# Registers one expert at a time, turns in banks of their own, and one schedule as written

## The chip, the cores and the metric

The kernel runs on one core of a Trainium2 chip. The metric is the device time of one execution in microseconds.

## What is computed

Attention in chunks of 64 tokens, then a layer with 8 experts of which each token takes one, then a layer with 4 experts that all tokens pass, weighted. All in float32:

```python
attn = softmax(q_c @ k_c.T / sqrt(64)); out = attn @ v_c   # 2 x 8 heads x 9 chunks of 64
x = out as (1152, 512)
expert_idx = argmax(x @ w_gate)                            # 8 experts, capacity 288 each
disp[e, place] = x[i]                                      # i in order, dropped when full
y = relu(disp @ w1) @ w2                                   # 512 -> 1024 -> 512, per expert
out[i] = gate_w[i] * y[expert_idx[i], pos[i]]              # kept tokens
h = relu(x @ w1[e]); out += p[:, e] * (h @ w2[e])          # second layer, 4 experts, all tokens
```

## The kernel before

**Numbers.** Every float32 product is made of three products of a high part and a low part (`hl`, `xt`, `ht`: [0] high, [1] low). ACT makes the high part by a cast, DVE the low one by a subtraction (for weights `part_hi`, L115, and `part_lo`, L119).

**Attention** (L125 to L449). Tokens go in 9 tiles of 128; the loop over `j` (L323) works on stages of four tiles at once: scores of tile j, weights and values of j−1, the transposed x and logits of j−2, the rank of j−3. `fetch` (L151) brings a tile's keys, queries and values from `kqv_d`: tile 0 in three transfers, each later tile in one of 768 KB. All tiles' fetches go out in order from SP's queue. `put_k` scales the keys into `kb`; ACT does so for one half of tile 2. At its end the routing (L390 to L447) works out, on DVE, how many tokens each expert keeps and where they start (`ovi`: the number kept, then for 8 places in turn the form, then the 8 offsets), the indices for the gathers (`gidx`), and `over`. `form` tells how many row blocks an expert needs. After it `warm` matmuls (L138) keep TensorE busy.

**Registers** (L548). `numbers` loads some words of a tile into registers of the engines. L551 and L552 load all of `ovi` once, `kept` and the 8 forms on every engine, the 8 offsets on ACT and DVE. Since the expert part has no order of its own at the border, its loads stand among the last operations of the routing on DVE.

**Experts** (L520 to L735). `expert(k)` calls itself for k+1 inside a condition on `form_r[k+1]` (L728, "more"). One expert has up to three row blocks, in the order w=1 (128 rows, if form > 2, L677), w=2 (64 rows, if form is 2 or 3, L682 and L683) and w=0 (128 rows, always). A `block` (L560) is: `first(0)` into bank `pg0[w]`, `first(1)` into `pg1` with `turn(0)` in its midst, `second(0)` into `y` with `turn(1)` in its midst, `second(1)`, and at the end four transposes `ty`. A turn transposes `hs`, the array's result that ACT copied out; ACT then writes the high part `ht` (L596) and DVE the low part (L597). The turns and `ty` take the two banks of tag "tp" in turn; `y` has two banks. `xprep` transposes the gathered tokens (`xr`) of the next expert between the products of block w=0, in banks `pg0[1]`, `pg0[2]` and `pg1`. `late(k)` (L639) puts four `part_lo` of this expert's last weights on DVE before the first block, and fetches the next weights into the raw tiles that they free.

With these inputs the experts at places k=0 to 5 run. Their blocks are: k=0 w=1 and 0; k=1 all three; k=2 w=0 alone; k=3 and k=4 w=2 and 0; k=5 w=0 alone.

**Second layer** (L735 to L877): 240 us to the end of the span, in which TensorE works without pause.

The order within attention is written out for all engines, and within the experts for PE, ACT, DVE and SP, each in a manual schedule of its own; at the border the two meet in an order that a scheduler chooses.

Of the kernel before, what the change touches and what calls it, by code (L numbers as in the profile page):

```python
# [9 lines left out]
F32 = mybir.dt.float32  # L10
# [8 lines left out]
ENG = mybir.EngineType  # L19

P = 128
NTOK = 1152
# [4 lines left out]
DM = H * D  # L27
KD = DM // P
# [43 lines left out]
def kernel(ctx: ExitStack, tc: tile.TileContext, kqv_d, wg, w_all, dp, cst, out, cap):  # L72
# [4 lines left out]
    assert cap <= XW  # L77

    dpool = ctx.enter_context(tc.tile_pool(name="dpool", bufs=1, space=DRAM))
    x_d = dpool.tile([NTOK, DM], F32, name="x_d")  # L80
# [44 lines left out]
    with ExitStack() as ast:  # L125
        ap_ = ast.enter_context(tc.tile_pool(name="attn", bufs=2))
        ps = ast.enter_context(tc.tile_pool(name="aps", bufs=1, space=PSUM))
        ast.enter_context(tc.manual_schedule())

# [20 lines left out]
        def fetch(i):  # L150
            if i < NT:  # L151
                kqv[i] = ap_.tile([P, 3, DM], F32, tag="kqv", bufs=KQV, name="kqv")
                if i == 0:
                    for t in range(3):
                        nc.sync.dma_start(out=kqv[i][:, t], in_=kqv_d[:, i, t])
                else:
                    nc.sync.dma_start(out=kqv[i], in_=kqv_d[:, i])
# [361 lines left out]

    with ExitStack() as est, tc.manual_schedule(engines={ENG.PE, ENG.Activation, ENG.DVE, ENG.SP}):  # L520
        hp_ = est.enter_context(tc.tile_pool(name="mh", bufs=2))
        xtp = est.enter_context(tc.tile_pool(name="mx", bufs=1))
        ps = est.enter_context(tc.tile_pool(name="mps", bufs=1, space=PSUM))

        ys2 = [ps.tile([P, DM], F32, name=f"y{j}") for j in range(2)]


        pg0 = [ps.tile([P, FH], F32, name=f"pg0{j}") for j in range(3)]
        pg1 = ps.tile([P, FH], F32, name="pg1")
        xts = [xt0, xtp.tile([P, 2 * KD * XW], F32R, name="xt1")]  # L530
        xbig = [x[:, 0:4 * KD * P].rearrange("p (a k n) -> p a k n", a=2, k=KD) for x in xts]
# [18 lines left out]

        kept, *form_r = numbers(ovi[0:1, 0:1 + NE], max_val=NTOK)  # L551
        o_r = numbers(ovi[0:1, 1 + NE:1 + 2 * NE], engines=(ENG.Activation, ENG.DVE), max_val=NTOK)  # L552
        regs = []
# [6 lines left out]
        def block(k, w, also=()):  # L560
# [4 lines left out]
            both = n < P  # L565
            y = ys2[w % 2]
            hs, ht = {}, {}
# [23 lines left out]
            def turn(h):  # L591
                tp = ps.tile([P, NF, n], F32, tag="tp", bufs=2, name="tp")
                for j in range(NF):
# [30 lines left out]
            yr = hp_.tile([P, DM], F32, tag="ys", bufs=1, name="yr")  # L624
            ty = ps.tile([P, KD, n], F32, tag="tp", bufs=2, name="tp")
            for j in range(2):
# [24 lines left out]
        def expert(k):  # L651
# [3 lines left out]
            if k == 0:  # L655
# [6 lines left out]
                for kd in range(KD):  # L662
                    xprep(0, kd, ps.tile([P, 512], F32, tag="tp", bufs=2, name="tp") if kd < 2 else (pg0[0], pg1)[kd - 2])
                for h in range(2):
# [9 lines left out]
            elif k + 2 < NE:  # L674
                gather(k + 2)
            late(k)
            with tc.If(form_r[k] > 2):  # L677
                block(k, 1)
# [20 lines left out]
            def nxt(i, kd):  # L699
                if k + 1 < NE:  # L700
                    t = pg1 if len(turns) == KD else pg0[1 + len(turns) % 2]
                    turns.append(t)
# [20 lines left out]
            block(k, 0, also)  # L723
            if k == 0:
                scatter(meta_d, [(posi[:, i:i + 1], meta[:, i]) for i in range(NT)], [])
                nc.gpsimd.dma_start(out=mcol, in_=meta_d.rearrange("(i p) c -> p i c", p=P))
# [7 lines left out]

    with ExitStack() as est, tc.manual_schedule(engines={ENG.PE, ENG.Activation, ENG.DVE, ENG.SP}):  # L735
        accp = est.enter_context(tc.tile_pool(name="accp", bufs=1))
# [132 lines left out]
        def pick_last(ws):  # L869
            if len(ws) == 1:  # L870
                return dense(ws[0])
            with tc.If(kept <= LAST + ws[0]) as few:  # L872
                dense(ws[0])
# [48 lines left out]
```

## Time and profile before

| | us |
|---|---|
| median of 3 runs | 619.68 |
| lowest and highest | 617.58, 619.73 |
| the profiled execution's own time | 620.28 |
| its span, first to last instruction | 618.1 |
| PE busy | 579.5 (94%) |
| DVE busy | 296.1 (48%) |
| ACT busy | 200.9 (32%) |
| mean granted TensorE clock | 0.975 |

The span lies 2.2 us inside the profiled execution's time. Busy shares are means over the attention (to about 60 us), the experts (to 240 us) and the second layer. A wait is put down to what came last: an engine's name with a q (DVEq, PEq) stands for its sequencer, which takes branches and sets semaphores, apart from the arithmetic. The granted clock is a share of full speed: 1.00 is 2.4 GHz, 0.50 is 1.2 GHz.

### The profile page before, as it was taken

What the parts mean: (1) busy time and instruction counts of PE and PEld (TensorE: products, weight loads), DVE (VectorE), ACT (ScalarE), POOL (GpSimd) and SP (SyncE); (2) the same over time, 40 slices, a digit from 0 to 9 for tenths busy, and PEclk for the clock granted to TensorE, in tenths of its full rate; (3) what the DMA queues carried; (4) which work ended last, traced back from release to release, by engine and by line L of the source; (5) the groups of instructions that cost most, each with busy time, mean ns of one, the idle gap of its engine ahead of it and who ended that gap; (6) DMA issues with size and microseconds to landing.
All of it is one profiled execution on the core that took longest, in us unless ns stands there. A gap on an engine that the chain in (4) does not pass through costs nothing.

```text
span 618.1 us, 8796 instructions
## 1 busy us (share of the span) xinstructions
PE 579.5 (94%) x3376; PEld 503.6 (81%) x3376; DVE 296.1 (48%) x576; ACT 200.9 (32%) x394; POOL 71.5 (12%) x63
## 2 busy tenths in 40 slices
PE   6998699998797988999999999999999999999995
PEld 3785577776676767989989989989989989989984
DVE  4897828147445376242462452452452452454221
ACT  4785237267454476111211211211211211211110
POOL 3311813202202050000000000000000000000032
PEclk8997799999898999999999999999999999999998
DMA  8782286428727176400120120120220000000022
GB/s 326 258 286 75 60 315 202 114 73 296 262 69 249 46 233 200 186 1 1 68 69 1 68 69 1 69 68 1 69 68 1 2 1 1 1 0 1 1 83 76
DMA packets 17322, 61.36 MB, mean 99 GB/s; under 512 B 2720, under 2 KB 2864, under 8 KB 16624
## 3 DMA queue, kind: packets, MB, share of 16 engines
q1 hardware_dynamic: 14544, 52.95, 25.1%
q0 software_dynamic: 2720, 7.66, 4.1%
q8 instruction: 33, 0.54, 0.4%
q14 instruction: 25, 0.20, 0.1%
HBM read 55.86 MB, written 4.75 MB: 98 GB/s over the span
## 4 chain that ended last, share of the span: by engine, by line
PE 59%; issue 1%; POOL 1%; DVE 0%; POOLq 0%
PE pg L768 30%; PE po L797 20%; PE po L816 8%; POOL out L500 1%; PE po L831 0%; DVE xr L804 0%; POOLq L872 0%; POOLq L500 0%
## 5 line engine op out<-in xcount | busy, mean ns | idle before, releaser
L768 PE MATMUL pg<-x,hl 128*128 128x384 f32 (+1 forms) x1152 | 187.5, 322 | 1.6 <-DVEq L728 1.6
L768 PEld LDWEIGHTS pg<-x,hl 128*128 128x128 f32 x1152 | 184.5, 188 | 3.1 <-issue 1.8
L797 PE MATMUL po<-hl,h 128*128 128x512 f32 (+1 forms) x588 | 137.4, 392 | 0.0
L797 PEld LDWEIGHTS po<-hl,h 128*128 128x128 f32 x588 | 108.6, 188 | 24.6
L119 DVE TENSOR_TENSOR hl<-raw,hl 128x1024 fp32r<-128x1024 f32 x80 | 95.3, 1219 | 24.0 <-ACT hl L115 20.2
L778 ACT ACTIVATE h<-pg 128x384 fp32r<-128x384 f32 x64 | 31.5, 492 | 186.1 <-PE pg L768 185.8
L115 ACT CAST hl<-raw 128x1024 fp32r<-128x1024 f32 x80 | 82.2, 1056 | 0.9 <-DVEq L728 0.9
L779 DVE SCALAR_TENSOR_TENSOR h<-pg,h 128x384 fp32r<-128x384 f32 x64 | 35.6, 557 | 94.2 <-ACT h L778 94.2
L574 PE MATMUL pg<-hl,xt 128*128 128x512 f32 x240 | 65.4, 421 | 3.2 <-PEq L682 1.6
L574 PE MATMUL y<-hl,ht 128*128 128x512 f32 x240 | 65.0, 412 | 1.6 <-DVE ht L597 1.6
L804 DVE SCALAR_TENSOR_TENSOR xr<-po,mcol,xr 128x512 f32<-128x512 f32 (+1 forms) x43 | 31.7, 737 | 59.7 <-PE po L797 59.0
L574 PEld LDWEIGHTS pg<-hl,xt 128*128 128x128 f32 x240 | 45.9, 200 | 14.6 <-issue 5.3
L574 PEld LDWEIGHTS y<-hl,ht 128*128 128x128 f32 x240 | 43.7, 192 | 13.4 <-DVE ht L597 4.4
L816 PE MATMUL po<-h,hl 128*128 128x288 f32 x384 | 51.9, 295 | 0.0
L816 PEld LDWEIGHTS po<-h,hl 128*128 128x128 f32 x384 | 51.3, 189 | 0.0
L775 ACT CAST h<-pg 128x288 fp32r<-128x288 f32 x32 | 12.8, 400 | 97.9 <-DVE pg L773 97.9
L400 POOL DMA_INDIRECT xr<-x_d,gidx x24 | 28.2, 1174 | 127.8 <-PE pg L540 95.4
L825 POOL MEMSET raw<- 128x512 f32 x1 | 0.5, 527 | 268.4 <-DVE hl L119 268.4
L597 DVE SCALAR_TENSOR_TENSOR ht<-tp,ht 128x512 fp32r<-128x512 f32 (+1 forms) x22 | 13.6, 616 | 28.5 <-ACT ht L596 28.4
L822 DVE TENSOR_TENSOR rest<-po,rest 128x288 f32<-128x288 f32 x28 | 12.8, 458 | 26.6 <-PE po L816 26.6
L773 DVE SCALAR_TENSOR_TENSOR pg<-pg,xt 128x288 f32<-128x288 f32 x32 | 22.1, 690 | 1.6 <-PE pg L768 1.6
L776 DVE TENSOR_TENSOR h<-pg,h 128x288 fp32r<-128x288 f32 x32 | 14.7, 459 | 15.4 <-ACT h L775 15.4
(158 smaller groups left out, 393.6 us busy)
## 6 DMA issues: line engine op xcount, KB each, us to landing
raw<-in_w_all SPq DMA_DIRECT2D x72, 512.0 KB, 4.1
kqv<-in_kqv SPq DMA_DIRECT2D x8, 768.0 KB, 8.1
raw<-in_w_all SPq DMA_DIRECT2D x4, 1024.0 KB, 5.7
x_d<-x SPq DMA_DIRECT2D x9, 256.0 KB, 3.1
xt<-meta_d SPq DMA_DIRECT2D x1, 1056.0 KB, 8.5
kqv<-in_kqv SPq DMA_DIRECT2D x3, 256.0 KB
xr<-x_d,gidx POOLq DMA_INDIRECT x24
cc<-in_cst SPq DMA_DIRECT2D x1, 373.5 KB
```

Source lines behind the costliest of these rows:

```text
L115: nc.scalar.copy(hls[j][:, 0, a:b], raws[j][:, a:b])
L119: nc.vector.tensor_tensor(out=hls[j][:, 1, a:b], in0=raws[j][:, a:b], in1=hls[j][:, 0, a:b].bitcast(F32), op=ALU.subtract)
L400: nc.gpsimd.indirect_dma_start(out=xrs[k % 2][0:n, w, :], out_offset=None, in_=x_d[:, :], in_offset=bass.IndirectOffsetOnAxis(ap=ix, axis=0))
L574: nc.tensor.matmul(o, t(a), wt(b), start=start and i == 0, stop=stop and i == len(pairs) - 1)
L768: nc.tensor.matmul(pg[:, 0:n], w1(u % 2, a, kd)[:, ff * P:ff * P + P], x2[:, b, kd, g * GW:g * GW + n], start=c == 0, stop=c == 3 * KD - 1)
L773: nc.vector.scalar_tensor_tensor(out=hs, in0=hs, scalar=0.0, in1=domain(u // NH), op0=ALU.max, op1=ALU.mult)
L776: nc.vector.tensor_tensor(out=h[:, ff, 1, 0:n], in0=hs, in1=h[:, ff, 0, 0:n].bitcast(F32), op=ALU.subtract)
L778: nc.scalar.activation(out=h[:, ff, 0], in_=pg[:, 0:GW], func=ACTF.Relu)
L779: nc.vector.scalar_tensor_tensor(out=h[:, ff, 1], in0=pg[:, 0:GW], scalar=0.0, in1=h[:, ff, 0].bitcast(F32), op0=ALU.max, op1=ALU.subtract)
L797: nc.tensor.matmul(po, h[:, ff, a, tt * P:tt * P + P], w2(u % 2, b, ff)[:, cols], start=c == 0, stop=c == 3 * NF - 1)
L804: nc.vector.scalar_tensor_tensor(out=acc[t][:, cols], in0=po, scalar=pe, in1=acc[t][:, cols], op0=ALU.mult, op1=ALU.add)
L816: nc.tensor.matmul(po[:, 0:W], w2(u % 2, b, ff)[:, d * P:d * P + P], h[:, ff, a, 0:W], start=c == 0, stop=c == 3 * NF - 1)
```

## The change

Line numbers of the kernel after are higher by 1 (L119 is L120) to 11.

1. One manual schedule over the whole kernel, so the border between attention and experts runs as written. POOL's manual schedule ends with the attention, as before.
2. Tile 1's keys, queries and values are fetched in three transfers of 256 KB, as tile 0's.
3. At first only `form_r[0]` is loaded, and the first offset is the number 0. `count(k + 1)`, after `late(k)`, loads one form on every engine and one offset on ACT and DVE. `kept` is loaded at the end of expert 0.
4. Three banks `tps` instead of the two rotating ones, and one `y` instead of two. The first turn and `ty` of a block take `tps[w]`, the second turn takes `pg0[w]`; `xprep` of the next expert takes `pg0[1]`, `pg0[2]`, `tps[1]`, `tps[2]`, `pg1`.

```diff
+    ctx.enter_context(tc.manual_schedule(engines={ENG.PE, ENG.Activation, ENG.DVE, ENG.SP}))
     dpool = ctx.enter_context(tc.tile_pool(name="dpool", bufs=1, space=DRAM))
...
-        ast.enter_context(tc.manual_schedule())
+        ast.enter_context(tc.manual_schedule(engines={ENG.Pool}))
...
-                if i == 0:
+                if i < 2:
                     for t in range(3):
                         nc.sync.dma_start(out=kqv[i][:, t], in_=kqv_d[:, i, t])
...
-    with ExitStack() as est, tc.manual_schedule(engines={ENG.PE, ENG.Activation, ENG.DVE, ENG.SP}):
+    with ExitStack() as est:
...
-        ys2 = [ps.tile([P, DM], F32, name=f"y{j}") for j in range(2)]
         pg0 = [ps.tile([P, FH], F32, name=f"pg0{j}") for j in range(3)]
+        tps = [ps.tile([P, 512], F32, name=f"tp{j}") for j in range(3)]
         pg1 = ps.tile([P, FH], F32, name="pg1")
+        y = ps.tile([P, DM], F32, name="y")
...
-        kept, *form_r = numbers(ovi[0:1, 0:1 + NE], max_val=NTOK)
-        o_r = numbers(ovi[0:1, 1 + NE:1 + 2 * NE], engines=(ENG.Activation, ENG.DVE), max_val=NTOK)
+        kept = []
+        form_r = [*numbers(ovi[0:1, 1:2], max_val=4)]
+        o_r = [0]
+
+        def count(k):
+            form_r.extend(numbers(ovi[0:1, 1 + k:2 + k], max_val=4))
+            o_r.extend(numbers(ovi[0:1, 1 + NE + k:2 + NE + k], engines=(ENG.Activation, ENG.DVE), max_val=NTOK))
...
-            y = ys2[w % 2]
...
-                tp = ps.tile([P, NF, n], F32, tag="tp", bufs=2, name="tp")
+                tp = (tps, pg0)[h][w][:, 0:NF * n].rearrange("p (f n) -> p f n", f=NF)
...
-            ty = ps.tile([P, KD, n], F32, tag="tp", bufs=2, name="tp")
+            ty = tps[w][:, 0:KD * n].rearrange("p (d n) -> p d n", d=KD)
...
-                    xprep(0, kd, ps.tile([P, 512], F32, tag="tp", bufs=2, name="tp") if kd < 2 else (pg0[0], pg1)[kd - 2])
+                    xprep(0, kd, (tps[0], tps[2], pg0[0], pg1)[kd])
...
             late(k)
+            if k + 1 < NE:
+                count(k + 1)
...
-                    t = pg1 if len(turns) == KD else pg0[1 + len(turns) % 2]
+                    t = (pg0[1], pg0[2], tps[1], tps[2], pg1)[len(turns)]
...
             block(k, 0, also)
             if k == 0:
+                kept.extend(numbers(ovi[0:1, 0:1], max_val=NTOK))
...
-            with tc.If(kept <= LAST + ws[0]) as few:
+            with tc.If(kept[0] <= LAST + ws[0]) as few:
```

In the program's order, DVE at the border between attention and experts, before (`hl_91` is the first expert's weights, `over` what TensorE waits for):

```order
L549 TENSOR_LOAD ovi
L918 BRANCH_PREFETCH_HINT
L441 TENSOR_TENSOR dt<-dt,thr 128x8
L442 TENSOR_TENSOR tsb<-tsb,dt 128x8
L549 TENSOR_LOAD ovi
L119 TENSOR_TENSOR hl_91<-raw_87,hl_91 128x1024
L443 TENSOR_TENSOR gp<-tsb,sel 128x192
L119 TENSOR_TENSOR hl_91<-raw_87,hl_91 128x1024
L445 TENSOR_REDUCE gidx<-gp 128x24
L447 TENSOR_TENSOR over<-n_ps,st 128x8
L536 TENSOR_TENSOR xt_71<-tp,xt_71 128x256 x2
```

and after (`hl_93` is the same weights):

```order
L442 TENSOR_TENSOR dt<-dt,thr 128x8
L443 TENSOR_TENSOR tsb<-tsb,dt 128x8
L444 TENSOR_TENSOR gp<-tsb,sel 128x192
L446 TENSOR_REDUCE gidx<-gp 128x24
L448 TENSOR_TENSOR over<-n_ps,st 128x8
L551 TENSOR_LOAD ovi
L120 TENSOR_TENSOR hl_93<-raw_89,hl_93 128x1024 x2
L538 TENSOR_TENSOR xt_73<-tp_1012,xt_73 128x256
L538 TENSOR_TENSOR xt_73<-tp_1014,xt_73 128x256
```

The loads and the two `hl` have left the chain from `dt` to `over` and stand behind it, one load in place of two.

TensorE in a 64-row block (k=1 and every later one), from the conditions to the first turn, before:

```order
L682 COMPARE_AND_BRANCH
L683 COMPARE_AND_BRANCH
L574 MATMUL pg_1011<-hl_91,xt_1013 128x512 [waits DVE_49]
L574 MATMUL pg_1011<-hl_91,xt_1013 128x512 x7
L574 MATMUL pg_1012<-hl_93,xt_1013 128x512 [waits DVE_49,Activation_49]
L574 MATMUL pg_1012<-hl_93,xt_1013 128x512 x3
L578 MATMUL tp<-cc,hs 128x64 [waits DVE_49,Activation_49]
L578 MATMUL tp<-cc,hs 128x64 x3
```

and after:

```order
L692 COMPARE_AND_BRANCH
L693 COMPARE_AND_BRANCH
L582 MATMUL pg_1011<-hl_93,xt_1017 128x512 [waits DVE_49]
L582 MATMUL pg_1011<-hl_93,xt_1017 128x512 x7
L582 MATMUL pg_1015<-hl_95,xt_1017 128x512 [waits DVE_49,Activation_49]
L582 MATMUL pg_1015<-hl_95,xt_1017 128x512 x3
L586 MATMUL tp_1014<-cc,hs 128x64 [waits Activation_49]
L586 MATMUL tp_1014<-cc,hs 128x64 x3
```

The turn no longer waits for DVE. In the 128-row block w=0 the wait for DVE moves from the turn to the transposes of `xr` into `pg01` and `pg02` (1010 and 1011 there).

TensorE between two experts (k=1 to k=2), before:

```order
L580 MATMUL tp<-cc,yr 128x128
L728 COMPARE_AND_BRANCH
L918 BRANCH_PREFETCH_HINT
L677 COMPARE_AND_BRANCH
L574 MATMUL pg_1010<-hl_91,xt_71 128x512 [waits DVE_49]
```

and after:

```order
L588 MATMUL tp_1012<-cc,yr 128x128
L739 COMPARE_AND_BRANCH
L551 TENSOR_LOAD ovi
L929 BRANCH_PREFETCH_HINT
L687 COMPARE_AND_BRANCH
L582 MATMUL pg_1010<-hl_93,xt_73 128x512 x7
```

One load of a register stands between the two conditions, at every later border too; at the border before k=1 a second one (`kept`) stands ahead of the first condition.

## Rows read from the trace of the kernel before

**Rows 1.** the page, part 4: the longest chain's share of the span by line

```profile
PE pg L768 30%; PE po L797 20%; PE po L816 8%; POOL out L500 1%; PE po L831 0%; DVE xr L804 0%; POOLq L872 0%; POOLq L500 0%
```

**Rows 2.** the chain in order of time, first long piece (start, us, what)

```profile
240.21 16.88 PE pg L768 x96
```

**Rows 3.** waits of PE: waited for, us in total, times, longest us

```profile
PE tp L540 <- DVE over L447: 5.0, 1, 5.0
PE tp L578 <- DVEq L677: 4.5, 2, 2.3
PE s_ps L206 <- DVE kb L168: 4.0, 1, 4.0
PE tp L580 <- DVEq L682: 2.7, 2, 1.4
```

**Rows 4.** timeline, attention: start us, us, engine, line, operation [idle before <- releaser]

```profile
9.49 0.86 DVE L168 TENSOR_SCALAR kb<-kqv 64x512 f32<-64x512 f32 x2 [2.25 <-DMA kqv<-in_kqv]
...
11.29 0.63 ACT L166 ACTIVATE kb<-kqv 64x512 f32<-64x512 f32 x1 [2.26 <-DMA kqv<-in_kqv]
```

**Rows 5.** timeline of DVE at the seam, 57 to 80 us

```profile
60.90 0.17 DVE L441 TENSOR_TENSOR dt<-dt,thr 128x8 f32<-128x8 f32 x1 [1.26 <-issue]
...
63.09 1.22 DVE L119 TENSOR_TENSOR hl<-raw,hl 128x1024 fp32r<-128x1024 f32 x1 [1.82 <-issue]
...
65.90 0.15 DVE L447 TENSOR_TENSOR over<-n_ps,st 128x8 f32<-128x8 f32 x1
67.45 0.81 DVE L536 TENSOR_TENSOR xt<-tp,xt 128x256 fp32r<-128x256 f32 x2 [1.40 <-ACT xt L535]
...
77.03 0.68 DVE L597 SCALAR_TENSOR_TENSOR ht<-tp,ht 128x512 fp32r<-128x512 f32 x1
```

**Rows 6.** timeline of PE in the same stretch

```profile
77.77 1.43 PE L574 MATMUL y<-hl,ht 128*128 128x512 f32 x5 [1.41 <-DVE ht L597]
```

**Rows 7.** the register loads of L549: count, duration ns min/median/max, first and last start

```profile
L549 ACTq TENSOR_LOAD <-ovi x2: 987/1381/1775, 59.6 to 60.7; - x2
L549 DVEq TENSOR_LOAD <-ovi x2: 1119/1500/1880, 59.6 to 61.1; - x2
L549 SPq TENSOR_LOAD <-ovi x1: 767/767/767, 59.6 to 59.6; - x1
L549 PEldq TENSOR_LOAD <-ovi x1: 1042/1042/1042, 59.6 to 59.6; - x1
```

**Rows 8.** timeline of PE, the 64-row blocks of k=3 and of k=4

```profile
158.63 3.30 PE L574 MATMUL pg<-hl,xt 128*128 128x512 f32 x12 [0.57 <-issue]
164.21 1.76 PE L578 MATMUL tp<-cc,hs 128*128 128x64 f32 x8 [2.27 <-DVEq L677]
...
167.58 1.21 PE L574 MATMUL y<-hl,ht 128*128 128x512 f32 x4
...
198.69 1.91 PE L574 MATMUL y<-hl,ht 128*128 128x512 f32 x4
...
201.96 2.38 PE L574 MATMUL y<-hl,ht 128*128 128x512 f32 x8
```

**Rows 9.** windows: length, busy (PE, PEld, DVE, ACT, POOL), granted clock, DMA share, GB/s

```profile
199.00:202.00 3.00, 3.00 (x13) 2.61 (x12) 0.00 (x0) 0.57 (x1) 0.00 (x0) 0.51 0.39 157
```

**Rows 10.** timeline of DVE before the skips of k=2 and of k=3

```profile
142.39 4.62 DVE L119 TENSOR_TENSOR hl<-raw,hl 128x1024 fp32r<-128x1024 f32 x4
...
159.38 4.62 DVE L119 TENSOR_TENSOR hl<-raw,hl 128x1024 fp32r<-128x1024 f32 x4
```

**Rows 11.** timeline of all engines, k=2

```profile
148.89 0.69 DVE L597 SCALAR_TENSOR_TENSOR ht<-tp,ht 128x512 fp32r<-128x512 f32 x1
...
149.74 0.47 PE L574 MATMUL y<-hl,ht 128*128 128x512 f32 x1
```

**Rows 12.** the attention's load of one register (L364)

```profile
L364 SPq TENSOR_LOAD <-e0i x1: 533/533/533, 26.7 to 26.7; - x1
```

**Rows 13.** L677 within 142 to 146 us, DVE's sequencer

```profile
L677 DVEq COMPARE_BRANCH  x1: 62/62/62, 143.7 to 143.7; - x1
```

More of the change, by code (lines that the diff above doesn't have):

```diff
@@ L732 @@
         late(NE)
-    with ExitStack() as est, tc.manual_schedule(engines={ENG.PE, ENG.Activation, ENG.DVE, ENG.SP}):
+    with ExitStack() as est:
         accp = est.enter_context(tc.tile_pool(name="accp", bufs=1))
```

## Prediction

> **What bounds the kernel now.** I read the chain of waits first. Its list by line [rows 1] gives 58% of the span to three lines of TensorE in the last part (L768, L797, L816), and its first long piece [rows 2] starts at 240.21 us. From there on the chain is matmuls end to end and the diff does not touch their order, so what the change does has to happen before 240.21 and then shifts everything behind it one for one. Next I read what TensorE waits for [rows 3]. Four waits in the first 240 us are named by things that the change moves: 5.0 us for DVE's `over` (L447) at the seam between attention and experts, 4.5 us in two turns of 64-row blocks and 2.7 us in two turns of 128-row blocks, both ended by DVE's sequencer (its conditional skip of a block, not an arithmetic result), and 4.0 us for `kb` in the attention. 16 us in all, 2.6% of the time. The four places in order:
>
> *Attention.* TensorE's first scores of tile 1 wait for DVE's `kb`, which itself waited 2.25 us for tile 1's fetch [rows 4]. ACT waits at 11.29 for the fetch of tile 2, 2.26 us, with the next `et` copy queued behind it.
>
> *Seam.* On DVE [rows 5] holes of 1.26 us before the second `dt` and of 1.82 before an `hl` subtraction stand in the chain to `over`, which ends at 66.05; then DVE works nearly without a hole to 77.71 (`ht`). On TensorE [rows 6] the first product of the second layer starts at 77.77, having waited 1.41 us for that `ht`. So the seam ends on DVE's queue. The holes are the register loads: those of L549 [rows 7] took 1.12 and 1.88 us on DVE, and 1.04 us on TensorE.
>
> *Expert k=3 and k=4.* Their 128-row second block is not run, the 64-row block is. TensorE has 12 products in the first 3.30 us, then sits 2.27 us for DVEq at the first turn, and everything up to the second turn is slow after it [rows 8]: 4 products took 1.91 us at k=4, where the 12 of k=3 took 3.30. The windows [rows 9] show why: behind the hole of k=4 the granted clock is 0.51, the lower level of 1.2 GHz. DVE meanwhile has four `hl` subtractions to 164.00 [rows 10]; its sequencer signals the skip only then, and the turn starts at 164.21.
>
> *Expert k=2 and k=5.* Only the last block runs. Here `ht` ends at 149.58 on DVE and `y` starts at 149.74 [rows 11], so the turn's wait of 1.4 us covers little: 0.16 us is all that an earlier turn gives.
>
> **The change part by part.**
>
> *Tile 1 in three fetches.* Gain: keys land before values, so `kb` and scores(1) can start by up to the 2.25 us that DVE waited [rows 4]. But tile 2's fetch goes out later by two more issues on SP, and ACT's copy of tile 2's keys stands in the queue before tile 1's `et`. I take +0.8 us; ends: −0.7 (nothing gained, tile 2 that much later) and +1.8 (most of the 2.25).
>
> *One schedule as written, seam.* The load leaves the place between the two `dt`; the chain `dt`, `dt`, `tsb`, `gp`, `gidx`, `over` now runs without the two loads and the two `hl` between. Of the 66.05, the holes of 1.26 and 1.82 us that DVE spent on the loads go, and the two `hl` of 1.22: 60.5; I take 61.0 for the end of `over`, as its last operands may come late too. Behind it come one register load, the two `hl` that were ahead (2 x 1.22 us), which fill the 1.40 us for which DVE then waited for `xt`, and the same work as before: 66.05 to 77.71 is 11.66. So `ht` ends at 61.0 + 0.8 + 2.4 + 11.66 − 1.40 = 74.5, or 75.6 with a load of 1.9; 2.1 to 3.2 us earlier. TensorE gets one more load before its first products, inside its 1.41 us of slack. Its hole before `y` may grow to 3 us, and the windows [rows 9] show what a hole does to the clock, so I take +1.9; ends −1.0 and +3.2.
>
> *Registers one expert at a time.* This is the added cost. TensorE now has a load between the branch compare and the first product of each of experts 1 to 5, two of them at k=1 (`kept` and the next count). For one register on TensorE no row exists. Bounds from the rows: SP's one-register load took 0.53 [rows 12], TensorE's nine registers 1.04, DVE's slower one 1.88 [rows 7]. SP's nine registers took 0.77, so eight more cost 0.23; TensorE's 1.04 less that is 0.8, which I take, being nearest to the same engine. At k=1 nothing hides it: two loads, less what the end of the transposes covers, −1.3 (−0.6 to −3.4). At k=2 and k=5 it falls into the turn's 1.4 us of waiting. At k=3 and k=4 it falls into the 2.27 us. On DVE and ACT there are two loads per expert, between the four `hl` and the next compare. I cost them at nothing, since the sequencer goes ahead of the arithmetic: DVE's compare of L677 at k=2 ran at 143.7 [rows 13], while the four `hl` ran to 147.01 (142.39 + 4.62 [rows 10]), 3.3 us for two loads of 0.8. If that cover is gone, the price is the rival below.
>
> By the Trainium skill's "Runtime: NRT & Kernel Launch" (Instruction fetch mechanics) a register load costs about 200 ns a register; the trace shows 29 ns a register on SP, 0.77 against 0.53 us, so the measurement decides, and by that page one register for each load would cost TensorE a quarter of what I take and the sum would be 2 x 0.6 = 1.2 us better (the two loads of k=1, the only ones that nothing covers). "DMA: Bandwidth & Descriptors" (Latency and other measured facts) of the Trainium skill gives such a load a floor of about 600 ns; SP's 533 here is a little under it, and by that floor the sum would be 0.4 us better.
>
> *Other banks for the turns.* The first turn of a 64-row block no longer shares its bank with what DVE reads in the skipped block; it waits for ACT alone. At k=3: products start 158.63 + 0.8 = 159.4 and take 3.30, the turn comes at 162.7 instead of 164.21, and its `ht` on DVE can be written right after the skip, 164.2 + 0.42 = 164.65. `y` starts near 164.7 instead of 167.58, and the clock has no 2.27 us hole in front of it. +3.0 after paying the load (ends +1.7 and +3.3). At k=4 the clock stayed low longer: `y` near 195.7 instead of 198.69, and its second half at 197.1 instead of 201.96 [rows 8]. +4.6 (+3.3 to +4.9). In 128-row blocks the wait for DVE goes from the turn to the two `xr` transposes four and twelve instructions later (banks `pg01`, `pg02` are then the skipped block's), and `ht` on DVE is the limit anyway: +0.15 each for k=2 and k=5 (−0.5 to +0.2). Expert k=1 runs all blocks and gains nothing here. The attention's and the dense part's rows are otherwise the same.
>
> *Sum.* +0.8 +1.9 −1.3 +0.15 +3.0 +4.6 +0.15 = 9.3 us, against the profiled run's own 620.28: 611.0. That run is 0.6 above the median of the three, so for the median: **610.4**.
>
> **The rivals.**
>
> *Loads cost 1.9 us* (the slower ones of ACT and DVE, for eight registers, 0.77 for nine on SP: the number of registers isn't what made them slow, and several engines load at once here too). Then k=1 is −3.4; at k=3 and k=4 the turn slips to 164.3 and its like, 0.5 more than the skip's signal, +2.5 and +4.1; at k=2 and k=5 the products end 0.5 after the old wait, −0.5 each; the seam +1.0. With the attention's 0.8 that is 4.0 us, 615.7 for the median, on the edge of what can be told from no change. Against it: five of the seven loads in [rows 7, 12] took 1.12 us or less. Chance 0.13.
>
> *DVE's loads wait for the work ahead of them* (ends slower). Each expert has two loads between the four `hl` and the skip's signal. If they wait till the `hl` are done, `ht` is late by two loads in every expert, on the path at k=1, k=2, k=5 and the seam, and it eats the gain of k=3 and k=4. At 0.9 us each that is −2.1 in sum (621.8); at 1.9 each, −14 (634). It decides slower from about 1.0 us a load. For it: at the seam `dt` started 1.26 us late behind a load, so a load does hold what follows it on DVE. Against it: the compare at 143.7 [rows 13] went ahead of running arithmetic. Chance 0.12.
>
> *The wait only moves.* At k=3 and k=4 the bank's wait could come back at the next user: the second turn now takes `pg0[w]`, the bank of the first product. That one is read out by ACT for `hs` before the first turn, so it is free; and `ht` on DVE ends 2.9 us before the old `y`. If all the same only the skip's signal counts and the clock still falls, k=3 and k=4 give 1 us each and the sum is 3.7: 616.0. Chance 0.07, on the same edge.
>
> *The change does nothing in its attention or seam part* (the gathers, not `over`, end TensorE's wait): the sum loses up to 2.7 and stays faster, 613.1. It lies in the forecast's range.
>
> **How the numbers follow.** 0.5% is 3.1 us, about what a measurement of this kernel tells from no change. The forecast with its bounds (low end: loads of 0.5, attention +1.8, seam +3.2, 606.5) has 0.68, all of it faster. The two cases on the edge split: loads of 1.9 into 0.06 faster and 0.07 same, the moved wait into 0.04 and 0.03. The drained DVE is the same at its mild end, 0.04, and slower for 0.08. So faster 0.78, same 0.14, slower 0.08. The range reaches to 617.5, which holds the forecast with all its bounds and the first and third rival with what they may miss by, and leaves out the drained DVE.
>
> **What would show it.** Right: TensorE's waits list no longer has DVEq L677 (L687 after) at 64-row turns, the granted clock stays 1.00 through k=3 and k=4, `over` ends near 61.0, and dense starts near 231. Loads on TensorE near 0.8 us. Wrong: loads of 1.5 us or more; DVE's compare later than the end of its four `hl`; a hole in front of `y` at k=3 longer than 1 us; a low clock in the seam longer than before; tile 2's scores later than before.

## The result, and the profile after

| | before | after |
|---|---|---|
| median, us | 619.09 (4 runs, 617.58 to 619.73) | 609.30 (4 runs, 608.57 to 612.56) |
| profiled execution, us | 620.28 | 609.62 |
| its span, us | 618.1 | 607.8 |
| mean granted clock | 0.975 | 0.987 |

The ratio of after to before is 0.9856, 95% interval 0.9814 to 0.9897: 1.4% faster, 9.8 us by the medians. The forecast was 610.4, in a range of 606.5 to 617.5.

To see where it came from, two kinds of marks serve that stand in the same place in both programs (the seam is the border between attention and experts, a border the stretch between two experts): the start of `n_ps`, the product with which the attention's last counts end, and the start of the four transposes `ty` that end each expert. The stretches between them, from the two timelines of TensorE (the gain is before less after; the last column is the term of the prediction):

| stretch | before, us | after, us | gain | forecast |
|---|---|---|---|---|
| attention, to `n_ps` | 56.42 | 56.25 | +0.17 | +0.8 |
| routing's end, seam, expert k=0 | 43.51 | 40.06 | +3.45 | +1.9 |
| k=1 | 40.43 | 40.87 | −0.44 | −1.3 |
| k=2 | 16.99 | 16.56 | +0.43 | +0.15 |
| k=3 | 30.94 | 28.35 | +2.59 | +3.0 |
| k=4 | 32.41 | 28.27 | +4.14 | +4.6 |
| k=5 | 17.19 | 17.64 | −0.45 | +0.15 |
| to the second layer's first product | 2.32 | 2.27 | +0.05 | 0 |
| second layer to the end | 377.89 | 377.53 | +0.36 | 0 |
| span | 618.1 | 607.8 | +10.3 | +9.3 |

The second layer starts 9.94 us earlier in the chain in order of time, against 240.21 in [rows 2]:

```profile
230.27 16.88 PE pg L779 x96
```

TensorE's waits after the change, in the columns of [rows 3]:

```profile
PE y L582 <- DVE ht L605: 4.9, 3, 2.7
PE pg L582 <- PEq L687: 3.1, 3, 1.1
PE tp L542 <- DMA xr<-x_d,gidx: 2.4, 2, 1.2
PE s_ps L207 <- DVE kb L169: 1.8, 1, 1.8
```

The 5.0 us for `over` and both rows of DVEq (4.5 and 2.7 us) are gone from TensorE's list. What took their place there is smaller: `ht` at the first product of `y` (4.9 in three places), the engine's own sequencer at the borders (PEq, 3.1), and at the seam the gathers.

The 64-row blocks on TensorE, which answer to [rows 8]:

```profile
155.42 3.06 PE L582 MATMUL pg<-hl,xt 128*128 128x512 f32 x12 [0.96 <-PEq L687]
158.31 1.06 PE L586 MATMUL tp<-cc,hs 128*128 128x64 f32 x8
159.18 1.18 PE L582 MATMUL pg<-hl,xt 128*128 128x512 f32 x4
161.41 1.20 PE L582 MATMUL y<-hl,ht 128*128 128x512 f32 x4 [1.05 <-DVE ht L605]
...
183.78 3.02 PE L582 MATMUL pg<-hl,xt 128*128 128x512 f32 x12 [0.97 <-PEq L687]
...
189.76 1.21 PE L582 MATMUL y<-hl,ht 128*128 128x512 f32 x4 [1.06 <-DVE ht L605]
```

Each piece now follows the last. The first turn starts 2.89 us after the first product, where it was 5.58 (158.63 to 164.21), and 4 products of `y` take 1.2 us in both; at k=4 they took 1.91. The granted clock is 1.00 there:

```profile
158.00:162.00 4.00, 2.95 (x18) 2.11 (x17) 2.76 (x4) 1.07 (x3) 0.00 (x0) 1.00 0.91 238
186.00:190.00 4.00, 2.94 (x17) 2.15 (x16) 3.11 (x4) 1.42 (x3) 0.06 (x1) 1.00 0.88 214
```

Only `y` waits on TensorE, 1.05 us, for `ht`. But the wait for DVE's skip has not gone from the block. It stands on ACT now, before the high part of `ht`:

```profile
160.51 0.38 ACT L604 ACTIVATE ht<-tp 128x256 fp32r<-128x256 f32 x1 [2.30 <-DVEq L687]
```

In the two blocks ACT waits 4.6 us for it, as long as TensorE did before (4.5). The gain is what TensorE does meanwhile: the turn and four more products, and no low clock behind a hole. The signal of the skip comes at the same place in both kernels (6.7 us after the last `ty`), and `y` starts 3.6 us behind it before and 1.0 us after. Why ACT waits is not shown; all blocks share the two buffers of `ht`, so these are the likely reason.

DVE in the same block, and its sequencer's rows of L687 (L677 before), which answer to [rows 10, 13]:

```profile
155.72 4.62 DVE L120 TENSOR_TENSOR hl<-raw,hl 128x1024 fp32r<-128x1024 f32 x4
160.92 0.43 DVE L605 SCALAR_TENSOR_TENSOR ht<-tp,ht 128x256 fp32r<-128x256 f32 x1 [0.59 <-ACT ht L604]
```

```profile
L687 DVEq COMPARE_BRANCH  x1: 63/63/63, 157.9 to 157.9; - x1
L687 DVEq EVENT_SEMAPHORE  x1: 21/21/21, 160.4 to 160.4; - x1
```

The compare runs at 157.9, after two register loads, while the four `hl` go on to 160.34. The loads are hidden on DVE as forecast.

The seam on DVE, which answers to [rows 5]:

```profile
59.59 0.17 DVE L442 TENSOR_TENSOR dt<-dt,thr 128x8 f32<-128x8 f32 x1
...
60.67 0.15 DVE L448 TENSOR_TENSOR over<-n_ps,st 128x8 f32<-128x8 f32 x1
61.07 2.36 DVE L120 TENSOR_TENSOR hl<-raw,hl 128x1024 fp32r<-128x1024 f32 x2 [0.25 <-issue]
63.81 0.81 DVE L538 TENSOR_TENSOR xt<-tp,xt 128x256 fp32r<-128x256 f32 x2 [0.38 <-ACT xt L537]
...
73.42 0.68 DVE L605 SCALAR_TENSOR_TENSOR ht<-tp,ht 128x512 fp32r<-128x512 f32 x1
```

and on TensorE, which answers to [rows 6]:

```profile
61.37 0.30 PE L542 MATMUL tp<-cc,xr 128*128 128x128 f32 x1 [1.24 <-DMA xr<-x_d,gidx]
62.84 0.90 PE L542 MATMUL tp<-cc,xr 128*128 128x128 f32 x3 [1.18 <-DMA xr<-x_d,gidx]
...
74.15 1.42 PE L582 MATMUL y<-hl,ht 128*128 128x512 f32 x5 [2.75 <-DVE ht L605]
```

`over` is done at 60.82, 5.2 us earlier, and a hole of 0.25 us stands where 3.08 us of holes stood. TensorE's wait for the tokens is now ended by the gathers' transfers, at 61.37 and 62.84. `ht` ends at 74.10 instead of 77.71.

The register loads, which answer to [rows 7]:

```profile
L551 ACTq TENSOR_LOAD <-ovi x14: 271/278/471, 59.5 to 211.6; - x14
L551 DVEq TENSOR_LOAD <-ovi x14: 300/308/556, 60.4 to 214.1; - x14
L551 SPq TENSOR_LOAD <-ovi x8: 274/279/303, 59.5 to 217.4; - x8
L551 PEldq TENSOR_LOAD <-ovi x8: 298/307/487, 59.5 to 210.8; - x8
```

A load of one word took 0.28 to 0.31 us by the medians. On ACT, DVE and TensorE the longest, 0.47 to 0.56 us, is the engine's first; SP's first stands in the attention (0.49 us at 25.2).

### The profile page after: what moved, and what is told of

Its sections match the earlier page's. It is cut to its first block, busy times and chain, and to the rows that moved or that the text cites. A ratio compares the mean times of both kernels' runs of the same rounds, so it can differ in the third digit from the quotient of the medians.

```text
span 607.8 us, 8836 instructions
## 1 busy us (share of the span) xinstructions
PE 574.0 (94%) x3376; PEld 499.4 (82%) x3376; DVE 296.0 (49%) x576; ACT 200.3 (33%) x394; POOL 70.5 (12%) x63
## 4 chain that ended last, share of the span: by engine, by line
PE 60%; issue 1%; POOL 0%; POOLq 0%; DVE 0%
PE pg L779 30%; PE po L808 21%; PE po L827 8%; POOL out L501 0%; PE po L842 0%; POOLq L929 0%; DVE xr L815 0%; POOLq L883 0%; POOLq L501 0%
## 5 line engine op out<-in xcount | busy, mean ns | idle before, releaser
L120 DVE TENSOR_TENSOR hl<-raw,hl 128x1024 fp32r<-128x1024 f32 x80 | 95.3, 1220 | 25.0 <-ACT hl L116 21.5
L582 PE MATMUL pg<-hl,xt 128*128 128x512 f32 x240 | 63.4, 413 | 5.6 <-PEq L687 3.1
L597 ACT COPY hs<-pg 128x512 f32<-128x512 f32 x22 | 13.0, 589 | 25.1 <-PE pg L582 16.4
```

The costliest lines, as they stand in the source:

```text
L120: nc.vector.tensor_tensor(out=hls[j][:, 1, a:b], in0=raws[j][:, a:b], in1=hls[j][:, 0, a:b].bitcast(F32), op=ALU.subtract)
L582: nc.tensor.matmul(o, t(a), wt(b), start=start and i == 0, stop=stop and i == len(pairs) - 1)
```

## The experiments

All are given by their stretches, in us, between the same marks. "Attention" depends on the execution more than on the kernel, as the second experiment shows, so the stretches behind it are what is compared.

| kernel | attention | to k=0's end | k=1 | k=2 | k=3 | k=4 | k=5 | border | second layer | span |
|---|---|---|---|---|---|---|---|---|---|---|
| before | 56.42 | 43.51 | 40.43 | 16.99 | 30.94 | 32.41 | 17.19 | 2.32 | 377.9 | 618.1 |
| after | 56.25 | 40.06 | 40.87 | 16.56 | 28.35 | 28.27 | 17.64 | 2.27 | 377.5 | 607.8 |
| after, again | 58.06 | 40.02 | 41.03 | 16.53 | 28.37 | 28.27 | 17.61 | 2.26 | 378.3 | 610.4 |
| one fetch | 55.62 | 40.02 | 41.00 | 16.56 | 28.36 | 28.24 | 17.67 | 2.26 | 378.2 | 607.9 |
| loads in front | 56.56 | 41.83 | 40.38 | 16.51 | 28.38 | 28.26 | 16.70 | 2.26 | 378.3 | 609.2 |
| old banks | 56.21 | 41.13 | 40.98 | 17.00 | 30.93 | 32.41 | 17.19 | 2.32 | 378.6 | 616.8 |
| banks only | 56.44 | 45.00 | 40.38 | 16.52 | 28.34 | 28.27 | 16.77 | 2.26 | 378.0 | 612.0 |
| schedule only | 57.39 | 41.83 | 40.41 | 16.99 | 32.50 | 30.85 | 17.20 | 2.31 | 378.0 | 617.5 |
| three loads | 58.14 | 39.98 | 43.97 | 18.82 | 31.47 | 28.58 | 18.94 | 2.26 | 378.5 | 620.7 |
| loads early | 56.64 | 41.23 | 40.98 | 16.57 | 28.35 | 28.23 | 16.72 | 3.85 | 379.1 | 611.7 |
| early, and `hl` later | 56.89 | 37.34 | 40.48 | 16.24 | 27.67 | 27.59 | 16.20 | 2.61 | 379.6 | 604.6 |
| `hl` later | 58.26 | 37.42 | 41.29 | 16.26 | 27.69 | 27.56 | 16.20 | 2.27 | 377.9 | 604.8 |
| `hl` later, `kept` early | 59.36 | 37.33 | 41.05 | 16.24 | 27.69 | 27.57 | 16.20 | 2.26 | 378.0 | 605.7 |

**One fetch.** The kernel after, with tile 1 in one transfer.

```diff
-                if i < 2:
+                if i == 0:
```

> The kernel after, with tile 1 fetched in one transfer again. After the change TensorE was 1.57 us ahead at scores of tile 5 (24.33 against 25.89) and only 0.17 us ahead at 30.27, with the granted clock at 0.50 from 26 to 28 us. Theory: the fetch's gain is given back there, since the low-clock stretch that stood at 10.9 to 14.1 us before only comes later; then the first product of the experts stays within 0.3 us of 64.25, the low clock is back near 11 to 14 us and gone from 24 to 30, and the span stays within 1 us of 607.8. Rival: the low clock at 24 to 30 us was a chance of that one execution and the fetch is worth its 1.5 us; then the first product comes near 65.7 and the span is near 609.3.

Measured: 609.50 us (ratio to before 0.9841, 0.9796 to 0.9886), span 607.9, the same as after. The attention was 0.63 us shorter, not longer, and the low clock stood at 26 to 28 us here too, not at 11 to 14: the span came as the theory had it, its cause did not, and the experts' first product, at 63.60, was 0.65 us earlier than after instead of within 0.3. Two windows of the kernel after, and the second of them with one fetch (columns as in [rows 9], the granted clock is the third number from the end):

```profile
13.00:16.00 3.00, 3.00 (x30) 1.73 (x26) 1.58 (x7) 1.72 (x6) 1.37 (x1) 1.00 1.02 425
26.00:28.00 2.00, 2.00 (x14) 1.61 (x14) 0.32 (x1) 1.22 (x2) 0.78 (x1) 0.50 0.64 125
```

```profile
26.00:28.00 2.00, 2.00 (x18) 1.92 (x18) 1.55 (x5) 1.53 (x5) 1.49 (x1) 0.50 0.75 180
```

**The kernel after, again.** Unchanged, beside two later kernels.

> The kernel after, unchanged, beside the next two: 608.5 to 610 us, span 607 to 608.5. If the low clock at 24 to 28 us is the change's doing it is there again, with scores of tile 5 near 24.3; if it was chance it is gone or elsewhere and the experts' first product comes 1 us earlier.

Measured: 611.94 us (609.74 to 613.70; ratio 0.9882, 0.9841 to 0.9922), span 610.4, more than expected. The experts' stretches repeat within 0.2 us, the attention is 1.81 us longer. The granted clock was low at 13 to 16 us, where it had been 1.00 in the first execution:

```profile
13.00:16.00 3.00, 3.00 (x20) 1.31 (x16) 1.53 (x6) 1.37 (x6) 1.49 (x1) 0.55 1.02 423
26.00:28.00 2.00, 2.00 (x20) 1.48 (x22) 1.41 (x8) 0.37 (x1) 0.00 (x0) 0.74 0.32 124
```

So the same program's attention moves by 1.8 us with where the low clock falls, and the fetch's effect, whatever its sign, lies inside that. It can't be told from nothing, and what sets the place of the low clock there stays open. Over all runs of the table, nine executions with three fetches took 56.2 to 59.4 us to `n_ps` and four with one took 55.6 to 57.4, so no gain is shown.

**Loads in front.** The kernel after, with all registers loaded once.

```diff
-        form_r = [*numbers(ovi[0:1, 1:2], max_val=4)]
-        o_r = [0]
...
+        kept0, *form_r = numbers(ovi[0:1, 0:1 + NE], max_val=NTOK)
+        o_r = numbers(ovi[0:1, 1 + NE:1 + 2 * NE], engines=(ENG.Activation, ENG.DVE), max_val=NTOK)
...
-            if k + 1 < NE:
-                count(k + 1)
```

> The kernel after, with all registers loaded at once again, but still behind over (one schedule as written). Single loads took 0.27 to 0.31 us after the change, where nine words had taken 0.77 to 1.12 and the second load of eight words 1.78 to 1.88. Theory: the price goes by the number of words, so DVE has 1.1 + 1.9 us of loads behind over in place of 0.56, the seam's ht ends 2.4 us later (near 76.5), and the five borders of the experts give back 0.3 us each, 0.6 at k=1, where TensorE waits: 1.2 to 1.5; span near 609. Rival: the loads of before were slow because several engines loaded beside transfers at 60 us; then they take 0.5 us each here too, the seam is 0.5 us later and the span is near 606.8.

Measured: 610.41 us (ratio 0.9855, 0.9810 to 0.9900), span 609.2. Its loads:

```profile
L551 DVEq TENSOR_LOAD <-ovi x2: 1105/1486/1868, 60.6 to 61.9; - x2
L551 PEldq TENSOR_LOAD <-ovi x1: 1045/1045/1045, 59.8 to 59.8; - x1
```

DVE's took 1.11 and 1.87 us, as in the kernel before, though they stand in another place of the program. They come at the same time as there, near 60 us, so this run alone can't tell words from moment. The kernel after does: one word at 59.5 to 60.4 us took 0.47 us on ACT, 0.49 on TensorE and 0.56 on DVE. The price goes by what is loaded; the rival, 0.5 us each here, falls. The seam takes 1.8 us more, k=1 0.5 less and k=5 0.9 less; k=2, k=3 and k=4 don't change. So one word at a time wins 1.8 at the seam and pays 1.4 later, of which 0.9 is a low clock at k=5; the medians (610.41 against 609.30 and 611.94) don't tell the two kernels apart.

**Old banks.** The kernel after, with the turns in two rotating banks and two `y`.

```diff
-                tp = (tps, pg0)[h][w][:, 0:NF * n].rearrange("p (f n) -> p f n", f=NF)
+                tp = ps.tile([P, NF, n], F32, tag="tp", bufs=2, name="tp")
...
-                    t = (pg0[1], pg0[2], tps[1], tps[2], pg1)[len(turns)]
+                    t = pg1 if len(turns) == KD else pg0[1 + len(turns) % 2]
```

> The kernel after, with the two rotating banks for the turns and two y banks as before. Theory: the banks carry most of the gain; the first turn at k=3 and k=4 waits for DVE's skip again (2 us each) with a low clock behind it, and the span is 6.5 to 8 us longer, 614.5 to 616. Rival: the experts gained because the loads moved what DVE has in hand at the border; then the turns wait less than 1 us and the span is 608 to 611.

Measured: 616.78 us (ratio 0.9958, 0.9934 to 0.9981), span 616.8. k=2, k=3 and k=4 take what they took before, to 0.01 us, and two waits are back:

```profile
PE tp L586 <- DVEq L687: 4.4, 2, 2.2
PE tp L588 <- DVEq L692: 1.9, 2, 1.0
```

The 4.4 us are those of [rows 3] almost to the tenth. The span is 9.0 longer, more than expected, since the seam took 1.1 us more, with a low clock (0.50 at 74 to 76 us), and the second layer 1.1 more.

**Banks only.** The kernel before, with the same new banks and nothing else.

```diff
-                tp = ps.tile([P, NF, n], F32, tag="tp", bufs=2, name="tp")
+                tp = (tps, pg0)[h][w][:, 0:NF * n].rearrange("p (f n) -> p f n", f=NF)
...
-                    t = pg1 if len(turns) == KD else pg0[1 + len(turns) % 2]
+                    t = (pg0[1], pg0[2], tps[1], tps[2], pg1)[len(turns)]
```

> The kernel before, with the new banks alone (old registers, old seam, one fetch). Theory: the seam stays (first product near 67.9), k=3 and k=4 gain what they gained after the change and up to 0.3 us more each since no load stands in front of the products: 2.6 + 4.1 + 0.6, and k=2 0.8; span 618.1 - 8 = 610. Rival: without the later schedule the DVE sequencer's skip comes earlier or later than after the change and the gain halves; span 614.

Measured: 613.68 us (610.63 to 616.30; ratio 0.9900, 0.9867 to 0.9933), span 612.0. k=2 to k=4 gain 0.47, 2.60 and 4.14: the same as in the kernel after, without its schedule or its loads; the rival falls. The 0.3 us more at k=3 and k=4 each that were expected without a load did not come, so the load had cost nothing there. At k=5, where no load stands in the border, they gain 0.42 as well. The seam took 1.5 us more than before: the clock was 0.55 at 80 to 83 us, behind a wait of 2.9 us for `ht` before `y`.

**Schedule only.** The kernel before, with one manual schedule over the program.

```diff
+    ctx.enter_context(tc.manual_schedule(engines={ENG.PE, ENG.Activation, ENG.DVE, ENG.SP}))
...
-        ast.enter_context(tc.manual_schedule())
+        ast.enter_context(tc.manual_schedule(engines={ENG.Pool}))
```

> The kernel before with one schedule over the whole program as the only change (all registers at once, old banks, one fetch). Theory: the seam gains what the run with loads in front kept of it, 1.5 us (first y after ht at 76.2 to 76.5 against 77.77), and the experts take what they took before: 16.8 us from k=2 to k=3, 31.0 for k=3, 32.7 for k=4; span 616.5 to 617. Rival: without the hl ahead of over the seam gains all of its 3.6 us, and the loads of nine words are hidden; span 614.5.

Measured: 619.69 us in one run, span 617.5. The seam gains 1.68, as the loads in front kept of it; the rival falls. The whole time is not told from that of before. The experts sum to what they took before (k=3 and k=4 together 63.35 in both kernels, but k=3 is 1.56 longer and k=4 as much shorter, with the low clock, 0.50 at 166 to 170 us, at k=3), and its attention ran 1.0 us longer than that of before.

**Three loads.** The kernel after, with two more loads of the form on TensorE.

```diff
             form_r.extend(numbers(ovi[0:1, 1 + k:2 + k], max_val=4))
+            for _ in range(2):
+                numbers(ovi[0:1, 1 + k:2 + k], engines=(ENG.PE,), max_val=4)
```

> The kernel after with three loads of the form on TensorE in place of one (two more at the seam and at each border, two checks of the value with each). Theory: at k=1 nothing covers a load, so its border is later by two loads, 0.6 us and the checks; at k=3 and k=4 the product y waits 1.05 us for ht on DVE whatever TensorE does, so two more loads of 0.3 us move the first product but not y; from k=2's start to k=5's the time stays within 0.3 us of 73.35. At k=5 the longer hole can keep the clock low a little longer. Rival: each load adds its 0.3 us at every border: k=2's start to k=5's takes 75.2.

Measured: 622.49 us in one run, span 620.7, 13 us more. From k=2's first product to k=5's it took 78.94 us: both theories miss. The timeline at k=3 and at k=4:

```profile
163.97 5.48 PE L584 MATMUL pg<-hl,xt 128*128 128x512 f32 x12 [2.34 <-PEq L689]
...
195.47 3.00 PE L584 MATMUL pg<-hl,xt 128*128 128x512 f32 x12 [2.38 <-PEq L689]
```

The hole in front of the first product grew by 1.4 us (0.96 and 0.97 in the kernel after), so one more load with its two checks costs TensorE 0.7. At k=4 that was hidden, as the theory has it: k=4 takes 28.58 against 28.27. At k=3 the 12 products took 5.48 instead of 3.06: the clock fell behind the hole, and likewise at k=1, k=2 and k=5. The forecast's argument, that a load at these borders falls into DVE's time, holds for the load, and fails for the clock, which fell behind four of the five holes that had grown so.

**Loads early.** The kernel after, with the loads of a border put into the block before.

```diff
-            if k + 1 < NE:
+            if k == 0:
...
+            if k == 0:
+                also[3].append(lambda: kept.extend(numbers(ovi[0:1, 0:1], max_val=NTOK)))
+            if k + 2 < NE:
+                also[3].append(lambda: count(k + 2))
```

> The kernel after with the next expert's registers and kept loaded in the midst of the block before (behind the fourth transpose group of block w=0), instead of at the border. Theory: the loads go under running products there, so the border at k=1 gives back its 0.84 us and the hole at k=5 its 0.4 us with the low clock behind it (18 products 4.4 us instead of 5.98, which the wait for ht limits to 0.5): dense starts at 229.0 instead of 230.27 and the span is 606.5. Rival: a load in the midst of a block holds TensorE's queue for 0.3 us each time and nothing is won: span 607.5 to 608.

Measured: 615.13 us (612.06 to 616.18), span 611.7. k=5 gives back its 0.92 us as expected. k=1 gains nothing, the seam took 1.2 us more with a low clock (0.50 at 76 to 78 us), and the last border is 1.6 us longer, with a wait that was not there before and slower products behind it (16.88 us in the kernel after):

```profile
PE pg L782 <- ACTq L742: 3.1, 1, 3.1
```

```profile
232.57 18.44 PE pg L782 x96
```

ACT's sequencer comes late to the second layer, and the granted clock is 0.50 at 234 to 236 us. The median lies 1.7 us above the profiled execution's 613.48, which no trace explains. Moving the loads moved a wait to an engine that the forecast for this kernel didn't look at.

**Early, and `hl` later.** The same, and the last two `hl` of a border put behind the first turn's `ht`.

```diff
-            with tc.If(form_r[k] > 2):
-                block(k, 1)
+            with tc.If(form_r[k] > 2) as big:
+                block(k, 1, [[], late3(k), [], [], [], [], []])
+            with big.Else():
+                for go in late3(k):
+                    go()
```

(`late3` holds `part_hi(3)`, `part_lo(3)` and the load of `late`'s second loop.)

> The same, and the subtractions for the last quarter of the weights (the second pair of the four hl at a border) moved behind the first turn's ht where block w=1 runs, in the other branch where it doesn't. At the seam ht then waits for two hl less: y, which waited 2.75 us for ht, starts 2.0 to 2.3 us earlier, near 72, and the clock has a hole of 0.6 us there instead. Theory: the seam ends on DVE's queue, so all of it reaches the end: span 604 to 604.5, 607.8 less 1.3 and 2.2. Rival: the two hl come back at the second turn or at the first products of the second half, and less than 1 us is won: span above 605.5.

Measured: 606.59 us (606.38 to 608.76; ratio 0.9808, 0.9757 to 0.9860), span 604.6. The seam's first `y` after the wait:

```profile
72.05 1.44 PE L582 MATMUL y<-hl,ht 128*128 128x512 f32 x5 [1.12 <-DVE ht L605]
```

It starts 2.1 us earlier than after the change and has waited 1.12 us instead of 2.75. The gain of 2.7 us in that stretch stays, and k=2, k=3 and k=4 gain 0.3, 0.7 and 0.7.

**`hl` later, alone.** The kernel after with the edit of the last run, and the registers as in the kernel after.

```diff
-            with tc.If(form_r[k] > 2):
-                block(k, 1)
+            with tc.If(form_r[k] > 2) as big:
+                block(k, 1, [[], late3(k), [], [], [], [], []])
```

> The kernel after with the last two hl of a border moved behind the first turn's ht (or into the other branch), the register loads left at the borders. Theory: the gain of the run with both was the moved hl (2.1 us at the seam and 0.5 to 0.8 us in each of k=2, k=3, k=4) and the early loads won 0.7 us at the border of k=1 and lost 1.5 us at the border to the second layer, where ACT's sequencer came late; so this one is a little faster than both together: span 603 to 604.5, 605 to 606 us. Rival: the early loads carried part of it, and the span is 605.5 or more.

Measured: 607.72 us (606.57 to 608.93; ratio 0.9824, 0.9792 to 0.9855), span 604.8 with an attention 1.4 us longer than in the run before. The time is above the 605 to 606 expected and not told from that of both together. k=5 gains 1.4 against the kernel after without any early load, which was not expected: the hole in front of its products is as long as there (1.29), but no low clock came behind it:

```profile
210.47 4.45 PE L582 MATMUL pg<-hl,xt 128*128 128x512 f32 x18 [1.28 <-PEq L698]
```

At k=3 ACT writes the high part of `ht` while DVE still works on its four `hl` (to 159.83), without waiting for the skip, and DVE's own part follows those at once, at 159.75:

```profile
158.97 0.38 ACT L604 ACTIVATE ht<-tp 128x256 fp32r<-128x256 f32 x1 [1.24 <-PE tp L586]
```

`y` starts 7.0 us behind the last `ty` there, 7.7 in the kernel after, and these are the 0.7 us of k=3. The early loads won 0.8 at k=1 and lost 0.3 at the last border and 1.7 in the second layer, where a low clock (0.50 at 227 to 229 us) followed as in the run with loads early.

**`hl` later, and `kept` alone early.** The last kernel, with one load moved.

```diff
-                kept.extend(numbers(ovi[0:1, 0:1], max_val=NTOK))
...
+                also[3].append(lambda: kept.extend(numbers(ovi[0:1, 0:1], max_val=NTOK)))
```

> The same with kept alone loaded in the midst of block w=0 of k=0, the forms at the borders. Theory: one of the two loads leaves the border of k=1, which gives 0.3 to 0.4 us, and the border to the second layer stays as it is in the kernel after (1.55 us): span 0.3 us less than the run without. Rival: it was the load of kept in the midst that made ACT late at the last border; then TensorE waits 3 us there again.

Measured: 606.79 us (605.63 to 607.64; ratio 0.9797, 0.9765 to 0.9829), span 605.7, not less than the run without, as its attention took 1.1 us more. k=1 gains 0.24 and the last border stays at 2.26, so `kept` was not what made ACT late. From `n_ps` to the end it takes 546.3 us, the least of all (after: 551.6; before: 561.7). In one series with it the kernel after took 611.94. By their medians the three versions with `hl` later beat both kernels.

## Why the prediction was right

The forecast missed the median by 1.1 us (the repeat's 611.94 lies 1.5 on the other side), and 9.3 of the 10.3 us of span were forecast. What it took for the likeliest course happened: TensorE's waits for DVE's sequencer went, and TensorE paid for loads. That the sum came so close is in part luck: by the table, gains put too low by 3.1 us (seam, k=1, k=2 and the stretches put at nothing) stood against gains put too high by 2.1 (attention, k=3, k=4, k=5). One sign of being wrong came, by a hair: the hole in front of `y` at k=3 was 1.05 us, where 1 was the limit. Point by point:

- **Banks, k=3 and k=4.** +3.0 and +4.6 forecast, +2.59 and +4.14 measured, and the runs with old banks and with banks only show that the banks alone make this. The step that was off by 0.4 each is "its `ht` on DVE can be written right after the skip, 164.2 + 0.42". It left out ACT, which must write the high part first and itself waits for the skip: the signal came at 160.4, ACT's part took 0.38 from 160.51, DVE's `ht` started at 160.92, 0.5 us after the signal, and `y` followed it.
- **k=2 and k=5.** The step "0.16 us is all that an earlier turn gives" failed. It took the end of `ht` on DVE as the earliest start of the first product of `y`, but only the second one needs that. At k=2 after the change, on TensorE and on DVE:

```profile
145.74 2.03 PE L582 MATMUL y<-hl,ht 128*128 128x512 f32 x6
```

```profile
145.59 0.68 DVE L605 SCALAR_TENSOR_TENSOR ht<-tp,ht 128x512 fp32r<-128x512 f32 x1
```

  `y` starts at 145.74, before DVE ends `ht` at 146.27: its first product reads only the high part, which ACT writes. The six products take 2.03 us, with the wait inside them. The banks gave 0.47 and 0.42 (banks only). At k=5 a longer border, with a low clock behind it, took more than that back:

```profile
212.37 5.98 PE L582 MATMUL pg<-hl,xt 128*128 128x512 f32 x18 [1.29 <-PEq L692]
```

```profile
214.00:218.00 4.00, 4.00 (x15) 3.18 (x14) 2.96 (x3) 0.98 (x2) 3.39 (x3) 0.75 0.80 197
```

  18 products took 5.98 us behind a hole of 1.29 us, with the clock at 0.75 of full from 214 to 218; 0.9 us of that is paid (17.64 against 16.70 with the loads in front). The second execution of the same kernel and the run with one fetch had it too (5.98 and 5.97), and yet a hole of 1.28 us at the same place had 4.43 to 4.45 behind it with the old banks and with `hl` later. So the hole alone does not decide, and what does stays open. "It falls into the turn's 1.4 us of waiting" counted a wait that the banks had removed; at k=2 the load cost 0.05 all the same (16.56 against 16.51).
- **Registers.** −1.3 at k=1 forecast, −0.44 measured (−0.57 to −0.60 in the repeat and with one fetch), −0.5 against the loads in front. The 0.8 us a load was too high. It rested on SP's 0.53 in [rows 12], by which eight words more seemed to cost only 0.23, and that was the engine's first load; first loads took 0.47 to 0.56 here, later ones 0.3. The hole at k=1 grew by 0.8 us with its two loads (first product 1.43 us after `ty`, against 0.61), and 0.4 came back behind it. That DVE's and ACT's loads cost nothing held at k=2, k=3 and k=4, which take within 0.05 us what they take with the loads in front.
- **Seam.** +1.9 forecast, +3.45 measured, repeated as 3.49 in two other runs. The mechanism was right and the size low: the load behind `over` held DVE 0.25 us instead of 0.8 or more, and what was set aside for a low clock (1.9 was taken where the sum gave 2.1 to 3.2) was not needed. The clock was low in the kernel before too, 0.50 from 66 to 72 us; in the kernel after it was 0.55 from 64 to 66 and 1.00 from 66 to 78, though the hole in front of `y` was 2.75 us. Half of the gain is the order (1.68, schedule only), half the smaller loads (1.77).
- **Attention.** +0.8 forecast, +0.17 measured, and not to be told from nothing. `kb` came 2.0 us earlier, as forecast (half of that came with one fetch too: 9.49 before, 8.45 with one fetch, 7.46 after), but TensorE's lead of 1.56 us at 24.3 us was down to 0.17 at 30.3, behind the low clock of 26 to 28 us.
- **The rivals.** Loads of 1.9 us: not for one word. DVE's loads waiting for the `hl`: the compare at 157.9 speaks against it. The wait that only moves: none at the second turn, but it did move to ACT's `ht`, where it costs less. The gathers: they end TensorE's wait at the seam now and leave DVE a hole of 0.38 us before `xt`; the rest up to `ht` is DVE's own work.
- **The range.** It does not hold the forecast with all its bounds, as it says: the worse ends of all terms together give 620.8, above 617.5, and the three named for its lower end give 607.4, not 606.5 (the better ends of all terms give 606.7).

## What to carry to other kernels

Where a block can be skipped at run time, a bank shared with it makes a running block wait for the other engine to reach and sign off the skip; a bank of its own takes the wait off that engine, and the low clock behind it can be worth nearly as much as the wait (k=4: a wait of 2.27 us gone, 4.14 us won). Look then for the next engine that waits for the same skip: here it was ACT, and the runs with `hl` later, in which ACT writes before DVE is through, win 0.7 us more in each of the two blocks. Load registers outside a chain of short dependent operations; one word at a time won 1.8 us in the chain and lost 1.4 at the borders, so count the hole that each load makes there. Before giving a wait a price, ask which operand the first instruction behind it reads: here the high part came earlier than the low one, and that decided 0.4 us twice.

## What was not expected of the hardware

- A second load of eight words took longer than a first of nine, on both engines that made it and in both places: 1.87 to 1.88 against 1.11 to 1.12 us on DVE. One word took 0.31. No run tells why.
- Holes of nearly the same length had different clocks behind them: 12 products took 5.48 us behind a hole of 2.34 us at k=3 and 3.00 us behind one of 2.38 us at k=4, in one execution. In front of `y` at the seam, 2.75 us (after) had a clock of 1.00 behind it and 2.1 us (old banks) one of 0.50.
- The place of a low clock in the first 32 us differs between executions of one program; the two that were traced differ by 1.8 us in their attention.
